# Pooled values in tiles of 112 and 32 partitions, a one-pass pooling of queries, and a new written order in an attention and mixture-of-experts kernel

## The chip, the cores and the metric

The kernel runs on one core of a Trainium2 chip. A core has five engines with instruction queues of their own: TensorE (PE in the profile, its weight loads PEld), VectorE (DVE), ScalarE (ACT), GpSimd (POOL) and SyncE (SP), which here issues all transfers. The metric is the device time of one execution in microseconds; less is better.

## The reference

Two batches of eight heads, 576 positions, head size 64, go through an attention with two branches, then through two feed-forward layers over 1152 tokens of width 512.

```python
q_d, k_d, v_d = (t.reshape(B, H, 144, 4, D).mean(axis=3) for t in (q, k, v))   # pooled by 4
out_d = softmax(q_d @ k_d.T / 8) @ v_d                                          # 144 x 144, no mask
out_up = np.repeat(out_d, 4, axis=2)
scores = np.where(abs(i - j) < 4, q @ k.T / 8, -1e9)                            # local window
x = (out_up + softmax(scores) @ v)            # -> tokens x 512
h = x @ w_in;  x = (h * sigmoid(h)) @ w_out   # 512 -> 2048 -> 512
p = domain_probs / domain_probs.sum(-1)
out = sum over e of p[:, e] * (relu(x @ w1[e]) @ w2[e])   # four experts, 512 -> 1024 -> 512
```

## The kernel before

The work is one long list of small steps, and TensorE does nearly all of the arithmetic in it. Attention comes as sixteen **jobs**, numbered 0 to 15 in the order batch, query half, pair of heads; jobs 0 to 3 and 8 to 11 have 256 queries per head in four blocks of 64, jobs 4 to 7 and 12 to 15 have 320 in five. Each step of a job has a letter, and a letter with a number is a step of one job: S local scores (fp32 matmuls of 64 rows by 64 columns and a mask added by an identity matmul), x maximum and subtraction, e exponential, k and q pooling of keys and queries, D pooled scores, n and d their maximum and exponential, u sums, r and g normalising, T transposes of the weights, a their copy out of PSUM, v pooling of the values on POOL, V the products with values, o the copy of the pooled part, f the sum of both branches, h and l the rounded high part and the low rest of the result (`xh`, `xl`), with which the products that follow work to nearly fp32 accuracy. The pooled queries past the last block are done per batch in one tail job (tp, tD, nt, dt, rt, gt, tT, ta).

In V the pooled keys are contracted, 144 of them. Before the change they lie as two halves of 72 partitions: `vg` is loaded as 72 rows of 4 KB, POOL adds four neighbours (two operations) into `vd`, and V contracts the halves kh = 0 and kh = 1 one after the other into the same PSUM columns, for each of two heads: four calls, each two fp32 passes (L483), before the calls of the local part (L487, 70 rows).

The weights of the first feed-forward layer come as 32 **pieces** of 512 KB (s0 to s31), of an encoding that three engines decode and split: A on ACT (two instructions, or one with the second, B, on DVE: `LOW_ON_DVE`), C on DVE, w the rounded copy (ACT, or DVE by `WHI_ON_DVE`), L the rest on POOL. Pieces 0 to 7 feed the first products (M and G, with th, gf, gh and gl after them), pieces 8 to 15 the second (H). The first token chunk (256 tokens) needs jobs 0 to 3, and its products H0 fill TensorE while jobs 4 to 7 are still on their way. `G1_0_0`, the first product of the second chunk, needs jobs 4 to 7. The experts' layer comes afterwards.

What sets the order: a scheduler by priorities, but over it the table `WRITTEN`, which gives for each engine a list of steps and adds an order between neighbours in it. An engine runs its instructions in that order and waits at the first that is not ready. Transfers are issued by SP in the order of the list as well, at most eight being under way, since they go round eight semaphores. Each step's PSUM tile is scarce: local scores have two, the transposes and V one each, products three.

Of the kernel before, what the change touches and what calls it, by code (L numbers as in the profile page):

```python
# [57 lines left out]
LOW_ON_DVE = (0, 3, 9, 13)  # L58
WHI_ON_DVE = (3, 4)
# [4 lines left out]
def attention_moe_kernel(ctx, tc, kqa, kqb, qtl, va, vb, w64, w1d, w2d, dpr, out):  # L64
# [350 lines left out]
    def down_scores(j):  # L415
        i = PE.matmul(out=j.ps[:, 352:352 + SD], lhsT=j.qd.rearrange("p a b -> p (a b)"), rhs=kd[j.b, j.hp],
                      start=True, stop=True)
        mark(f"D{j.i}", i)
        after(i, j.group)
# [27 lines left out]
    def trans(j):  # L447
        nb = j.nb
        if j.c == 1 and j.hp == 0:
            atd[j.b] = ac.tile([72, 2, NH, 80], F32, tag="atd1", name="atd1")  # L450
# [377 lines left out]
    def outputs(e, ci, ch, p):  # L828
# [36 lines left out]
        """S0 S1 D0 D1 S2 T0 S3 T1 V0 D2 D3 V1 M0 T2 V2 M1 T3 S4 V3 M2 D4 S5 M3 tD G0_3_0 G0_3_1 D5 G0_3_2 G0_3_3
        G0_4_0 G0_4_1 G0_4_2 T4 G0_4_3 G0_5_0 G0_5_1 G0_5_2 G0_5_3 G0_6_0 G0_6_1 G0_6_2 G0_6_3 S6 S7 tT G0_7_0
        G0_7_1 G0_7_2 G0_7_3 D6 V4 T5 H0_0_0 H0_1_0 D7 T6 V5 H0_2_0 H0_0_1 H0_1_1 H0_2_1 H0_0_2 H0_1_2 H0_2_2
        H0_0_3 V6 H0_1_3 H0_2_3 H0_0_4 H0_1_4 H0_2_4 H0_0_5 H0_1_5 T7 H0_2_5 H0_0_6 H0_1_6 H0_2_6 H0_0_7 H0_1_7
        H0_2_7 H0_3_0 H0_3_1 V7 H0_3_2 H0_3_3 H0_3_4 H0_3_5 H0_3_6 H0_3_7 G1_0_0 G1_0_1 G1_0_2 G1_0_3 G1_1_0
        G1_1_1 G1_1_2 G1_1_3 G1_2_0 G1_2_1 G1_2_2 G1_2_3 G1_3_0 G1_3_1 G1_3_2 G1_3_3 G1_4_0 G1_4_1 G1_4_2 G1_4_3  # L870
        G1_5_0 G1_5_1 G1_5_2 G1_5_3 G1_6_0 G1_6_1 G1_6_2 G1_6_3 G1_7_0 G1_7_1 G1_7_2 G1_7_3""",
# [226 lines left out]
```

## Time and profile before

| | |
|---|---|
| Runs of the kernel before, us | 675.71, 665.71, 662.03 (median 665.71) |
| Profiled execution | 659.74 us, of it span 657.7 us |
| Mean granted TensorE clock | 0.994 |
| Busy share: PE, PEld, DVE, ACT, POOL | 96%, 94%, 64%, 50%, 37% |

The span is what the profiler saw from the first to the last instruction; 2.04 us of the execution lie around it. All times of rows below count from the start of the span. Busy shares are means over stages with different limits, so the stages have to be looked at one by one.

### The profile page before, as it was taken

How to read it: one execution, taken by the hardware profiler on the slowest of the kernel's cores; microseconds unless marked ns; L12 is line 12 of the kernel's file. 1: busy time of each engine (PE TensorE's matmuls, PEld its weight loads, DVE VectorE, ACT ScalarE, POOL GpSimd, SP SyncE). 2: the span in 40 equal slices, each digit the busy share in tenths (PEclk: the TensorE clock that was granted, in tenths of full speed). 3: DMA queues.
4: the chain of work that ended last, by engine and by line, in shares of the span. 5: the costliest groups of instructions: out<-in, count | busy, mean ns of one | idle time of the engine just before them, and what ended most of it. 6: DMA issues, size and time to landing. Idle time of an engine off the chain costs nothing.

```text
span 657.7 us, 13693 instructions
## 1 busy us (share of the span) xinstructions
PE 630.2 (96%) x5484; PEld 616.3 (94%) x5484; DVE 418.8 (64%) x862; ACT 327.6 (50%) x744; POOL 245.3 (37%) x345
## 2 busy tenths in 40 slices
PE   4788999999999999999999999999999999999995
PEld 3677899999999999999999999999999999999995
DVE  6698465655545545766558956668954679755434
ACT  4789654568845434363345633346533356433321
POOL 5554651114510001653456322645522564333210
PEclk9899999999999999999999999999999999999998
DMA  9986512106612200240004310014300020000001
GB/s 260 328 283 181 170 54 73 26 5 196 191 59 65 65 1 1 65 161 1 1 1 129 97 33 2 1 34 129 97 1 1 1 65 1 1 33 33 1 33 50
DMA packets 16928, 48.17 MB, mean 73 GB/s; under 512 B 2976, under 2 KB 4256, under 8 KB 16864
## 3 DMA queue, kind: packets, MB, share of 16 engines
q1 hardware_dynamic: 16864, 47.29, 23.4%
q8 instruction: 43, 0.70, 0.5%
q14 instruction: 21, 0.17, 0.1%
HBM read 44.93 MB, written 2.36 MB: 72 GB/s over the span
## 4 chain that ended last, share of the span: by engine, by line
PE 79%; DMA 11%; DVE 3%; ACT 3%; POOL 2%; issue 1%; SPq 0%; ACTq 0%; POOLq 0%; DVEq 0%
PE mm L565 50%; PE p L794 26%; DMA stg<-in_w_dram 4%; DMA vg<-in_va_dram 2%; DMA acc<-in_kqa_dram 2%; DMA acc<-in_w_dram 2%; DMA qt<-in_qtl_dram 1%; DVE dec L230 1%; ACT stg L228 1%; PE t L455 1%; POOL vg L330 1%; ACT dec L222 1%; DMA kq<-in_kqa_dram 1%; PE o L487 1%; DVE acc L822 1%
## 5 line engine op out<-in xcount | busy, mean ns | idle before, releaser
L565 PE MATMUL mm<-xh,wbuf 128*128 128x256 f32 (+2 forms) x1280 | 263.8, 293 | 2.6 <-DVE gf L586 2.3
L565 PEld LDWEIGHTS mm<-xh,wbuf 128*128 128x128 f32 x1280 | 208.2, 188 | 4.1 <-DVE gf L586 3.3
L565 PE MATMUL mm<-xl,wbuf 128*128 128x256 f32 (+2 forms) x640 | 186.9, 292 | 0.0
L776 POOL TENSOR_TENSOR r<-r 128x128 f32<-128x128 f32 x160 | 95.3, 608 | 177.6 <-ACT r L770 136.2
L779 DVE TENSOR_TENSOR h<-r,h 128x384 fp32r<-128x384 f32 (+1 forms) x128 | 91.9, 719 | 64.5 <-ACT h L778 64.2
L778 ACT ACTIVATE h<-r 128x384 fp32r<-128x384 f32 (+1 forms) x128 | 73.7, 578 | 93.7 <-POOL r L776 54.2
L565 PEld LDWEIGHTS mm<-xl,wbuf 128*128 128x128 f32 x640 | 120.3, 188 | 0.0
L565 PE MATMUL mm<-gh,wbuf 128*128 128x256 f32 (+2 forms) x512 | 103.3, 295 | 0.3 <-DVE gf L586 0.2
L794 PE MATMUL p<-wext,h 128*128 128x256 f32 x672 | 89.4, 276 | 0.0
L565 PEld LDWEIGHTS mm<-gh,wbuf 128*128 128x128 f32 x512 | 82.2, 188 | 1.2 <-ACT acc L635 0.4
L794 PE MATMUL p<-wbuf,h 128*128 128x256 f32 x672 | 82.7, 276 | 0.0
L794 PEld LDWEIGHTS p<-wext,h 128*128 128x128 f32 x672 | 82.4, 188 | 0.0
L794 PEld LDWEIGHTS p<-wbuf,h 128*128 128x128 f32 x672 | 79.4, 188 | 0.0
L565 PE MATMUL mm<-gl,wbuf 128*128 128x256 f32 (+2 forms) x256 | 74.1, 292 | 0.0
L776 DVE TENSOR_TENSOR r<-r 128x128 f32<-128x128 f32 x96 | 39.3, 409 | 35.6 <-ACT r L770 31.2
L770 ACT ACTIVATE r<-mm 128x512 f32<-128x512 f32 x48 | 28.6, 597 | 65.3 <-PE mm L565 65.0
L565 PEld LDWEIGHTS mm<-gl,wbuf 128*128 128x128 f32 x256 | 48.1, 188 | 0.1
L592 DVE TENSOR_TENSOR gl<-gf,gh 128x256 fp32r<-128x256 f32 (+2 forms) x64 | 34.6, 543 | 17.9 <-ACT gh L591 17.5
L240 POOL TENSOR_TENSOR wbuf<-dec,wbuf 128x512 fp32r<-128x512 f32 x24 | 32.0, 1350 | 33.8 <-ACT wbuf L239 32.3
L591 ACT ACTIVATE gh<-gf 128x256 fp32r<-128x256 f32 (+2 forms) x64 | 28.1, 442 | 21.6 <-DVE gf L586 20.7
L822 DVE SCALAR_TENSOR_TENSOR acc<-p,pr,acc 128x256 f32<-128x256 f32 (+1 forms) x63 | 36.1, 604 | 3.5 <-PE p L794 3.0
L586 DVE SCALAR_TENSOR_TENSOR gf<-th,mm 128x256 f32<-128x256 f32 (+2 forms) x64 | 28.5, 451 | 14.9 <-ACT th L585 13.9
(138 smaller groups left out, 895.8 us busy)
## 6 DMA issues: line engine op xcount, KB each, us to landing
stg<-in_w_dram SPq DMA_DIRECT2D x25, 512.0 KB
kst<-in_w2d_dram SPq DMA_DIRECT2D x16, 512.0 KB
kst<-in_w1d_dram SPq DMA_DIRECT2D x12, 512.0 KB
acc<-in_w_dram SPq DMA_DIRECT2D x7, 512.0 KB
kq<-in_kqb_dram SPq DMA_DIRECT2D x8, 323.0 KB
kq<-in_kqa_dram SPq DMA_DIRECT2D x6, 419.0 KB
stg<-in_w1d_dram SPq DMA_DIRECT2D x4, 512.0 KB
vw<-in_vb_dram SPq DMA_DIRECT2D x8, 180.0 KB
```

The costliest lines, as they stand in the source:

```text
L222: first = ACT.activation(out=d, in_=v[:, :, 1].bitcast(F32), func=ACTF.Prelu, scale=2.0 ** -112, alpha=2.0 ** 32)
L240: mark(f"L{4 * u + j}", POOL.tensor_tensor(out=l[:, c], in0=d, in1=h[:, c].bitcast(F32), op=ALU.subtract))
L565: ins = [PE.matmul(out=ps, lhsT=l, rhs=r, start=(first and i == 0), stop=(last and i == n - 1)) for i, (l, r) in enumerate(pairs)]
L586: mark(f"gf{c}_{ft}", DVE.scalar_tensor_tensor(out=gf[:, 0:n], in0=th[:, 0:n], scalar=1.0, in1=ps[:, 0:n], op0=ALU.add, op1=ALU.mult))
L591: latest[ACT] = mark(f"gh{c}_{ft}", ACT.activation(out=gh[ft][:, 0:n], in_=gf[:, 0:n], func=ACTF.Copy))
L592: latest[DVE] = mark(f"gl{c}_{ft}", DVE.tensor_tensor(out=gl[ft][:, 0:n], in0=gf[:, 0:n], in1=gh[ft][:, 0:n].bitcast(F32), op=ALU.subtract))
L770: ACT.activation(out=r[:, 0:4].rearrange("p s t -> p (s t)"), in_=ps[:, 0:512], func=ACTF.Relu)
L776: latest[eng] = eng.tensor_tensor(out=r[:, o], in0=r[:, a], in1=r[:, b], op=op)
L778: ACT.activation(out=h, in_=r[:, part], func=ACTF.Copy)
L779: latest[DVE] = DVE.tensor_tensor(out=l, in0=r[:, part], in1=h.bitcast(F32), op=ALU.subtract)
L794: ins = [PE.matmul(out=ps, lhsT=x, rhs=y, start=(opens and k == 0 and i == 0), stop=(k == 3 and i == n - 1), skip_group_check=True) for i, ...
L822: DVE.scalar_tensor_tensor(out=o, in0=ps, scalar=p, in1=o, op0=ALU.mult, op1=ALU.add)
```

## The change

1. **Values.** `vg` and `vd` get 128 partitions. Of the first 72-row half of the load, the rows are cut in two halves of 2 KB that go to neighbouring partitions: rows 0 to 55 make partitions 0 to 111 (half 0), rows 56 to 71 make partitions 96 to 127 (half 1). That is two transfers for one, four POOL operations for two, and in V a call of 112 rows, then one of 32 rows, for each head. The exponential d writes its columns in the matching order, and the transposes of the pooled weights (L457, L470) become 128 columns wide.
2. **Queries of jobs 0 to 3.** One reduction over 128 partitions instead of two over 64; the pooled scores D of these jobs are two matmuls of 64 rows by 64 columns instead of one 128 by 128 with zeros in it.
3. **Who rounds what.** `LOW_ON_DVE` shrinks from pieces 0, 3, 9, 13 to piece 0; `WHI_ON_DVE` goes from 3, 4 to 2, 6, 9, 14, 15; a new table `WHI_ON_POOL` names 0, 3, 14.
4. **Order.** The load list and the four engine lists of `WRITTEN` are new.

```diff
-LOW_ON_DVE = (0, 3, 9, 13)
-WHI_ON_DVE = (3, 4)
+LOW_ON_DVE = (0,)
+WHI_ON_POOL = (0, 3, 14)
+WHI_ON_DVE = (2, 6, 9, 14, 15)
...
             if 4 * u + j in WHI_ON_DVE:
                 mark(f"w{4 * u + j}", DVE.tensor_copy(out=h[:, c], in_=d))
+            elif 4 * u + j in WHI_ON_POOL:
+                mark(f"w{4 * u + j}", POOL.tensor_copy(out=h[:, c], in_=d))
...
-            i = load(f"vg{j.i}", j.vg, va[j.b, j.hp, :, 0:1024])
+            for p, h, a in ((slice(0, 112), 0, slice(0, 56)), (slice(96, 128), 1, slice(56, 72))):
+                i = load(f"vg{j.i}", j.vg[p, 128 * h:128 * h + 128],
+                         va[j.b, j.hp, a, 0:1024].rearrange("p (k x) -> p k x", k=2))
...
-        for h in range(2):
-            p = slice(64 * h, 64 * h + 64)
-            mark(f"q{j.i}", DVE.tensor_reduce(out=j.qd[p, h], in_=q4[p], axis=AX.X, op=ALU.add))
+        mark(f"q{j.i}", DVE.tensor_reduce(out=j.qd, in_=q4, axis=AX.X, op=ALU.add))
...
-            mark(f"v{j.i}", fold(j.vg), padd(vf, j.vg[:, :, 0], j.vg[:, :, 1]))
+            for p, h in ((slice(0, 112), 0), (slice(96, 128), 1)):
+                g = j.vg[p, 128 * h:128 * h + 128]
+                mark(f"v{j.i}", fold(g), padd(v[p, h], g[:, :, 0], g[:, :, 1]))
...
+        if j.i < 4:
+            for h in range(2):
+                p = slice(64 * h, 64 * h + 64)
+                i = PE.matmul(out=j.ps[p, 352:352 + SD], lhsT=j.qd[p], rhs=kd[j.b, j.hp][p], start=True, stop=True)
...
-            mark(f"T{j.i}", PE.transpose(t2[0:72, 1 + kh], j.ed[:, 72 * kh:72 * kh + 72], ident))
+            mark(f"T{j.i}", PE.transpose(t2[:, 1 + kh], j.ed[:, 16 * kh:16 * kh + 128], ident))
...
-            for kh in range(2):
-                r = j.atd[:, kh, h, :] if j.c == 0 else atd[b][:, kh, 2 * hp + h, :]
-                mark(f"V{j.i}", PE.matmul(out=o[p, 320:320 + nd], lhsT=v[:, kh, p], rhs=r, start=(kh == 0), stop=(kh == 1)))
+            for kh, g in enumerate((slice(0, 112), slice(96, 128))):
+                r = j.atd[g, kh, h, :] if j.c == 0 else atd[b][g, kh, 2 * hp + h, :]
+                mark(f"V{j.i}", PE.matmul(out=o[p, 320:320 + nd], lhsT=v[g, kh, p], rhs=r, start=(kh == 0), stop=(kh == 1)))
...
-        """S0 S1 D0 D1 S2 T0 S3 T1 V0 D2 D3 V1 M0 T2 V2 M1 T3 S4 V3 M2 D4 S5 M3 tD G0_3_0 G0_3_1 D5 G0_3_2 G0_3_3
+        """S0 S1 D0 D1 T0 S2 V0 D2 S3 T1 M0 V1 T2 D3 S4 V2 M1 T3 S5 D4 V3 M2 T4 tD M3 D5 G0_3_0 G0_3_1 G0_3_2
...
-        """v0 v1 L0 L1 v2 v3 L2 L3 L4 p4 L5 L6 tp p5 L7 L8 L9 L10 p6 p7 L11 L12 L13 L14 L15""",
+        """v0 w0 L0 v1 v2 v3 L1 L2 w3 L3 p4 tp L4 L5 p5 L6 L7 L8 L9 p6 L10 L11 p7 L12 L13 w14 L14 L15""",
```

On TensorE the order of the first jobs before is this (L389 and L396 are S, L416 is D, L455 and L457 T, L483 and L487 V; tiles in these rows are named s scores, t transposed weights, o output):

```order
L416 MATMUL s<-kd,qbd_102 128x144
L416 MATMUL s<-kd,qbd_103 128x144
L389 MATMUL s<-kq_f 64x70 x8
L396 LDWEIGHTS ident_100
L396 MATMUL s<-mask,ident_100 128x280
L455 MATMUL t_233<-ident,sm 70x128 x4
L457 MATMUL t_234<-ident,ed 72x128 x2
L389 MATMUL s<-acc 64x70 x8
```

In the changed kernel the same place on TensorE reads so (L394 and L401 are S, L424 D, L467 and L469 T, L495 and L499 V):

```order
L424 MATMUL s<-kd,qs_102 64x144 x2
L424 MATMUL s<-kd,qs_103 64x144 x2
L467 MATMUL t_239<-ident,sm 70x128 x4
L469 MATMUL t_240<-ident,ed 128x128 x2
L394 MATMUL s<-kq_f 64x70 x8
L401 LDWEIGHTS ident_100
L401 MATMUL s<-mask,ident_100 128x280
L495 MATMUL o<-atd_249,vd 64x64 x4
L499 MATMUL o<-at,vw 64x64 x8
```

T0 has moved ahead of S2, and V0 ahead of S3, which is the first step to need the fourth load of keys and queries. A little later, likewise, S4 has come to stand ahead of V2, M1 and T3, behind which it stood.

On ScalarE before, this is the place at the end of the first batch: the two instructions of piece 14, then parts of pieces 16, 15 and 17, w14, o6, g7, w15, h6, a part of piece 18, and a7 (L458 to L465):

```order
L222 ACTIVATE dec<-stg_618 128x512
L228 ACTIVATE stg_618<-stg_618 128x512
L228 ACTIVATE stg_755<-stg_755 128x512
L222 ACTIVATE dec<-acc 128x512
L228 ACTIVATE acc<-acc 128x512
L228 ACTIVATE stg_823<-stg_823 128x512
L239 ACTIVATE wbuf<-dec 128x512
L490 ACTIVATE od<-o 128x80
L445 ACTIVATE ed<-ed,st 128x144
L239 ACTIVATE wbuf<-dec 128x512
L499 ACTIVATE xh<-o 128x320
L228 ACTIVATE stg_855<-stg_855 128x512
```

In the changed kernel the place on ScalarE between a6 and a7 holds gh0_6 and gh0_7 (L603), parts of pieces 16, 17 and 18 (L223, L229), g7 (L457) and o6 (L502):

```order
L603 ACTIVATE gh_648<-gf 128x256
L603 ACTIVATE gh_646<-gf 128x256
L229 ACTIVATE stg_769<-stg_769 128x512
L229 ACTIVATE stg_837<-stg_837 128x512
L457 ACTIVATE ed<-ed,st 128x144
L223 ACTIVATE dec<-stg_769 128x512
L229 ACTIVATE stg_869<-stg_869 128x512
L502 ACTIVATE od<-o 128x80
L470 ACTIVATE at<-t_1085 70x512
```

The copies w14 and w15 have left ScalarE, and piece 15 is done there well before; the parts of pieces 16 and 17 now come behind it.

On GpSimd the changed kernel has two of the rounding copies (CAST, L240), of pieces 0 and 3, among the values' pooling (L336) and the subtractions L (L243):

```order
L336 TENSOR_TENSOR vg_f_157<-vg_f_157 112x128x2
L336 TENSOR_TENSOR vd<-vg_f_157 112x128
L336 TENSOR_TENSOR vg_f_157<-vg_f_157 32x128x2
L336 TENSOR_TENSOR vd<-vg_f_157 32x128
L240 CAST wbuf<-dec 128x512
L243 TENSOR_TENSOR wbuf<-dec,wbuf 128x512
```

Before, the pooling was two rows of 72 partitions, and no CAST stood on GpSimd; no third one does now, for piece 14 stands in both tables and VectorE's is asked first.

## Rows read from the trace of the kernel before

**Rows 1.** The page, part 1: busy time of each engine.

```profile
PE 630.2 (96%) x5484; PEld 616.3 (94%) x5484; DVE 418.8 (64%) x862; ACT 327.6 (50%) x744; POOL 245.3 (37%) x345
```

**Rows 2.** Busy time by stage: stretch, its length, engines, then clock, DMA share, GB/s.

```profile
core 0: us, PE busy (x) PEld busy (x) DVE busy (x) ACT busy (x) POOL busy (x), PEclk, DMA share, GB/s
0.00:70.00 70.00, 51.05 (x588) 43.45 (x588) 53.06 (x134) 53.43 (x135) 38.49 (x57) 0.98 0.82 253
70.00:143.00 73.00, 72.75 (x809) 67.68 (x805) 42.04 (x120) 39.66 (x119) 20.71 (x43) 1.00 0.25 68
143.00:180.00 37.00, 35.92 (x257) 35.30 (x257) 21.91 (x35) 30.43 (x62) 18.43 (x14) 1.00 0.56 171
```

**Rows 3.** Waits of TensorE, 0 to 180 us: total, times, longest.

```profile
PE s L389 <- DMA kq<-in_kqa_dram: 4.2, 1, 4.2
PE s L389 <- DVE s L439: 3.6, 1, 3.6
PE mm L565 <- DVE gf L586: 2.5, 5, 1.0
```

**Rows 4.** TensorE in time: start, length, instruction, idle before it.

```profile
39.68 0.38 PE L565 MATMUL mm<-xh,wbuf 128*128 128x256 f32 x1 [0.43 <-DVE gf L586]
...
58.99 0.38 PE L565 MATMUL mm<-gh,wbuf 128*128 128x256 f32 x1 [0.17 <-DVE gf L586]
...
75.82 0.30 PE L565 MATMUL mm<-xh,wbuf 128*128 128x320 f32 x1
```

**Rows 5.** The chain that ended last, 105 to 123 us: start, length, what.

```profile
106.02 0.39 PE o L483 x8
106.41 0.47 PE o L487 x16
...
121.42 0.43 PE o L483 x8
121.85 0.58 PE o L487 x20
```

**Rows 6.** Stretches of 5 us while first loads run; columns as rows 2.

```profile
10.00:15.00 5.00, 1.36 (x18) 1.21 (x19) 4.65 (x15) 2.85 (x8) 2.20 (x3) 1.00 1.00 280
15.00:20.00 5.00, 4.54 (x54) 3.56 (x52) 3.77 (x8) 2.81 (x7) 2.89 (x3) 1.00 1.01 247
20.00:25.00 5.00, 3.15 (x46) 2.83 (x41) 4.23 (x15) 4.52 (x14) 2.46 (x4) 1.00 1.00 341
```

**Rows 7.** SyncE in time: the issue that had waited for job 4's load.

```profile
27.78 0.33 SPq L131 DMA_DIRECT2D vw<-in_vb_dram  x1
```

**Rows 8.** VectorE in time: pooling of queries, second decoding step, rounding copy.

```profile
4.21 0.84 DVE L359 TENSOR_REDUCE qbd<-kq 64x64 f32<-64x256 f32 x2 [3.35 <-POOL mask L267]
...
9.22 0.43 DVE L225 TENSOR_SCALAR stg<-stg 128x512 int32<-128x512 int32 x1 [0.19 <-DMA stg<-in_w_dram]
...
27.01 0.42 DVE L237 CAST wbuf<-dec 128x512 fp32r<-128x512 f32 x1
```

**Rows 9.** ScalarE in time.

```profile
15.07 0.66 ACT L228 ACTIVATE stg<-stg 128x512 int32<-128x512 uint16 x1
...
16.86 0.63 ACT L239 ACTIVATE wbuf<-dec 128x512 fp32r<-128x512 f32 x1
...
65.34 0.68 ACT L228 ACTIVATE stg<-stg 128x512 int32<-128x512 uint16 x1 [1.01 <-DMA stg<-in_w_dram]
```

**Rows 10.** From A5's start to a7's end on ScalarE; columns as rows 2.

```profile
28.81:69.31 40.50, 34.53 (x394) 30.30 (x392) 32.26 (x77) 36.34 (x94) 21.92 (x28) 0.96 0.75 234
```

**Rows 11.** GpSimd in time: pooling of values, a subtraction, pooling of queries.

```profile
7.46 1.04 POOL L330 TENSOR_TENSOR vg_f<-vg_f 72x512 f32<-72x512 f32 x1 [2.53 <-DMA vg_f<-in_va_dram]
8.58 0.64 POOL L330 TENSOR_TENSOR vd<-vg_f 72x256 f32<-72x256 f32 x1
...
14.44 1.29 POOL L240 TENSOR_TENSOR wbuf<-dec,wbuf 128x512 fp32r<-128x512 f32 x1
...
32.21 0.42 POOL L330 TENSOR_TENSOR kq<-kq 128x128 f32<-128x128 f32 x1 [1.07 <-PE s L389]
```

More of the change, by code (lines that the diff above doesn't have):

```diff
@@ L257, in attention_moe_kernel @@
     mask = ac.tile([128, 6, WIN], BF16, name="mask")
+    qs = [ac.tile([128, BQ], F32, name=f"qs{i}") for i in range(2)]
     qbd = [ac.tile([128, 2, BQ], F32, name=f"qbd{i}") for i in range(2)]
@@ L415, in down_scores @@
     def down_scores(j):
[L416 to L419, printed above, removed]
+        if j.i < 4:
+            for h in range(2):
+                p = slice(64 * h, 64 * h + 64)
+                i = PE.matmul(out=j.ps[p, 352:352 + SD], lhsT=j.qd[p], rhs=kd[j.b, j.hp][p], start=True, stop=True)
+                mark(f"D{j.i}", i)
+                after(i, j.group)
+        else:
+            i = PE.matmul(out=j.ps[:, 352:352 + SD], lhsT=j.qd.rearrange("p a b -> p (a b)"), rhs=kd[j.b, j.hp],
+                          start=True, stop=True)
+            mark(f"D{j.i}", i)
+            after(i, j.group)
     def tail_scores(l):
@@ L449, in trans @@
         if j.c == 1 and j.hp == 0:
-            atd[j.b] = ac.tile([72, 2, NH, 80], F32, tag="atd1", name="atd1")
+            atd[j.b] = ac.tile([128, 2, NH, 80], F32, tag="atd1", name="atd1")
         t1 = t_p.tile([128, 4, 128], F32, tag="t1", name="t1")
@@ L462, in trans @@
         else:
-            j.atd = ac.tile([72, 2, 2, 64], F32, tag="atd0", name="atd0")
+            j.atd = ac.tile([128, 2, 2, 64], F32, tag="atd0", name="atd0")
             dst = j.atd
-        mark(f"a{j.i}", ACT.activation(out=dst, in_=t2[0:72, 1:3].rearrange("p a (h q) -> p a h q", h=2), func=ACTF.Copy))
+        mark(f"a{j.i}", ACT.activation(out=dst, in_=t2[:, 1:3].rearrange("p a (h q) -> p a h q", h=2), func=ACTF.Copy))
     def tail_trans(l):
@@ L867, in attention_moe_kernel @@
[L867 to L871, printed above, removed]
@@ L872, in attention_moe_kernel @@
-        """tab e0 e1 A0 d0 d1 w0 g0 g1 A1 a0 w1 e2 e3 o0 a1 d2 h0 d3 A2 g2 o1 A3 h1 w2 a2 g3 A4 o2 A5 a3 h2 A6 e4
-        o3 w5 w6 h3 d4 A7 A8 th0_0 th0_1 g4 e5 th0_2 gh0_0 gh0_1 w7 th0_3 w8 gh0_2 dt0 d5 A9 gt0 th0_4 A10 w9 g5
-        gh0_3 a4 w10 gh0_4 A11 A12 e6 ta e7 th0_5 th0_6 w11 o4 d6 a5 h4 g6 A13 th0_7 gh0_5 d7 w12 o5 gh0_6 gh0_7
-        w13 h5 a6 A14 A15 w14 o6 g7 w15 h6 a7 ya0_0 ya0_1 ya0_2 o7 h7 ya0_3 th1_0 gh1_0 th1_1 gh1_1 th1_2 gh1_2
-        th1_3 gh1_3 th1_4 gh1_4 th1_5 gh1_5 th1_6 gh1_6 th1_7 gh1_7""",
@@ new lines, in attention_moe_kernel @@
+        H0_0_3 H0_1_3 V5 H0_2_3 T6 H0_0_4 H0_1_4 H0_2_4 H0_0_5 H0_1_5 H0_2_5 V6 T7 H0_0_6 H0_1_6 H0_2_6 H0_0_7
+        H0_1_7 H0_2_7 H0_3_0 H0_3_1 H0_3_2 H0_3_3 V7 H0_3_4 H0_3_5 H0_3_6 H0_3_7 G1_0_0 G1_0_1 G1_0_2 G1_0_3
+        G1_1_0 G1_1_1 G1_1_2 G1_1_3 G1_2_0 G1_2_1 G1_2_2 G1_2_3 G1_3_0 G1_3_1 G1_3_2 G1_3_3 G1_4_0 G1_4_1 G1_4_2
+        G1_4_3 G1_5_0 G1_5_1 G1_5_2 G1_5_3 G1_6_0 G1_6_1 G1_6_2 G1_6_3 G1_7_0 G1_7_1 G1_7_2 G1_7_3""",
+        """tab e0 A0 e1 d0 g0 d1 A1 a0 e2 g1 o0 h0 d2 a1 A2 w1 g2 o1 e3 A3 a2 A4 h1 d3 g3 o2 A5 e4 h2 a3 w4 w5 d4
```

42 lines of the change are left out of this document (23 added, 19 removed).

## The prediction

> **What bounds the kernel now.** I read the page's busy times first: TensorE is busy for 630.2 of 657.7 us [rows 1], so 27.5 us of idle time is all that any reordering can win. The table by stage says where it lies [rows 2]: 70.00 − 51.05 = 18.95 us in the first 70 us, 0.25 us in the next 73, 1.08 us up to 180. From 70 us on TensorE is the bound, and what is added to it there is added to the end. Before that it waits. The waits name causes of several kinds [rows 3]: 4.2 us for the very first load, which no order shortens, 3.6 us for VectorE's normalising of job 0, 2.5 us in five pieces for VectorE's first gate step. So the most that this change can win is 18.95 − 4.2 = 14.8 us, 2.2% of the profiled execution's 659.74 us, and only with a TensorE that never waits after its first load.
>
> The feeder that is nearest to full is ScalarE. Between the start of A5 (28.81) and the end of a7 (69.31), the last copy that TensorE needs of the first batch, it is busy 36.34 of 40.50 us [rows 10]: 4.16 us idle, 1.01 us of it in one wait for a load that stands ahead of w14, g7 and w15 [rows 9]. Gains on VectorE and GpSimd count only where they let ScalarE start earlier or wait less. After a7, TensorE has 6.5 us to `G1_0_0` at 75.82 [rows 4], and from there on runs without a gap worth counting.
>
> **The change part by part.**
>
> *Loads of values.* From 10 to 20 us, where three of the four vg loads and most of the 72-row vw loads run, 280 and 247 GB/s arrive; from 20 to 25 us, with loads of 128 rows, 341 [rows 6], at a DMA share of 1.0 in both. At 341 the 2.64 MB of those 10 us would take 7.7, so the narrow loads cost at most 2.3 us; vg carries two thirds of the narrow bytes (288 KB against 144 each), which leaves 1.5 us to this edit. The lower end is below nothing: vg now takes two of the eight places under way and four more issues at about 0.33 us [rows 7], in a row where SP is not the bound; I put it at −0.5. I take 1.0 us earlier for the loads behind the fourth vg, nearer to the upper end because the engines' share was full. The Trainium skill (DMA: Bandwidth & Descriptors, why a DMA increments its semaphore by 16) says that a transfer uses the largest number of engines up to 16 that divides both row counts: 12 for 72 rows, 14 for 56 pairs of rows, 16 for 32. By it the busiest engine's share of a vg falls from 24 to 20 KB, an estimate of a sixth less; by that share the loads would come 0.5 us earlier instead of 1.0, and the sum would be 660.6. No row here separates engines.
>
> *VectorE.* A pair of query reductions takes 0.84 us for 64 partitions each [rows 8]; one over 128 partitions has as many elements in a lane as one of them, so 0.42: −1.7 us for four jobs. Second decoding steps of pieces 3, 9, 13 leave (−3 × 0.42), five rounding copies stand for two (+3 × 0.42): nothing.
>
> *ScalarE.* It takes three decoding steps (+3 × 0.66) and hands over five copies (−5 × 0.63) [rows 9]: −1.2 us in all, but all of that before A5. Inside the stretch from A5 to a7, w4 comes in and four copies go (6, 9, 14, 15), two decoding steps come in, and a first step of piece 16 has moved ahead of a7: −3 × 0.63 + 3 × 0.66 = +0.1, nothing. So the stretch is 36.3 us of work again.
>
> *GpSimd.* A pooling of values was 1.04 + 0.64 us; in two parts it is twice the price of 256 and of 128 elements, 2 × (0.64 + 0.42) = 2.1 [rows 11]: +0.4 us for each of eight, hidden while GpSimd is idle for 31.5 of the first 70 us [rows 2]. No row shows its copy of 512 elements. Above, it can't reasonably exceed the two-input subtraction of that size, 1.29; below, VectorE's 0.42. I take 1.0, and it stands where w on ScalarE took 0.63: w0 then reaches M0 well before h0 and l0 do, and w3 is needed only by M3. The third copy doesn't happen on GpSimd: piece 14 is in both tables, and VectorE's is asked first. That costs VectorE 0.42, counted above. Without this cover (L0 late for M0) the price would be some 0.6 us once.
>
> *The order, walked.* I went through both lists with durations of like rows. Job 0 is normalised before the second exponential maximum and the third query, so T0 comes some 3 us earlier; V0 no longer stands behind S3 and its load, and M0 starts near 19.5. Next S4 now stands ahead of V2, M1 and T3. It needs job 4's load, which by SP's next issue had landed at 27.78 [rows 7]; with the loads 1.0 us earlier it lands near 26.7, about when V2 could start anyway, for V has one PSUM tile and waits for l1. A5 then starts near 28.1, 0.7 us earlier. From there ScalarE finds its inputs ready in nearly all places: pieces 12 to 15 land long before their turn, and the parts of pieces 16 and 17 come after piece 15 and at a time when their loads are in. With no idle time a7 would end at 28.1 + 36.3 = 64.4, 4.9 us earlier; with all of the old 4.16 us, 0.7 us earlier. My walk leaves out the hand-overs between engines, so I take half of the idle time as won: 0.7 + 2.1 = 2.8, rounded to 3.0 us, which TensorE passes on to `G1_0_0` since its own part after a7 is as long as before. On the way it finds `G0_3_0` about 2 and the third product of H0 several us earlier than 39.68 and 58.99 [rows 4], so TensorE isn't the late one in this stage.
>
> *The two calls in V.* This is added on TensorE. A V block of 8 passes with 64 columns took 0.39 us, the block behind it, of the same 128-row by 64-column shape, 0.47 for 16 [rows 5]: 0.029 a pass, so 8 cost 0.235 and entering the shape 0.155. With 80 columns, 0.43 − 8 × 0.036 = 0.14. So a change of tile shape costs about 0.14 to 0.155 us. Calls of 112 rows and of 32 now alternate, which is four changes in each V that weren't there. At 0.155 that is 0.6 us a job; at the low end some of it is the late second weight load, which a call of two passes doesn't suffer, and 0.1 remains: 0.4 us. Below that, nothing, if a 32-row call counts as no change of shape. I take 0.42. V4 to V7 lie where TensorE has slack while ScalarE is late; V8 to V15 lie after 70 us, on the bound: +8 × 0.42 = 3.4 us. The Trainium skill (TensorEngine Tiling (Array Packing), Tiling Modes, key properties) says that a change of tiling mode drains TensorE, and lists 32 rows as a mode apart from 128; no row here shows these two in turn, and by that rule the price isn't zero. The sum doesn't rest on it.
>
> *The rest.* D of jobs 0 to 3 is two small matmuls in quarters that don't overlap, in a time when TensorE waits; at worst it enters a shape once more, 4 × 0.15 us in slack. Wider transposes stream the same 128 columns of the identity. The changed column order of the exponential writes as many elements. For these I count nothing; if strided writes cost ScalarE a tenth of a microsecond each, eight of them lie in the stretch and take 0.8 from the gain.
>
> *Sum.* 659.74 − 3.0 + 3.4 = 660.1 us for a profiled execution. The runs shown lie higher: 662.03 and 665.71 and one far off; their median is 6.0 above the profile, the mean of the lower two 4.1. I take 4, nearer to the two runs that agree: **664 us**.
>
> **The rivals.**
>
> *V costs nothing more.* If a 32-row call behind one of 112 costs no change, 3.4 us come off, and with all idle time of ScalarE won another 1.9: 660.1 − 5.3 = 654.8, 659 as a median. For it: the call needs only the last quarter of the rows. Against it: each entry into another shape in the rows had a price. Chance 0.20.
>
> *V at its full price: slower.* The place is V8 to V15, the price 0.6 us each, 4.8 together, and V4 to V7 add 2.4 as soon as TensorE and not ScalarE is the late one. With the 3.0 won before, it decides from 3.0 / 8 = 0.38 us a job; with 0.7 won it ends at 659.74 − 0.7 + 7.2 = 666.2, 670 as a median. Chance 0.22.
>
> *S4 waits instead of V2.* If the loads aren't earlier, S4 stands until 27.8 with V2, M1 and T3 behind it, V2 begins 1.8 us later than in my walk, and o2, A5 and all of ScalarE's stretch follow: the 3.0 shrinks to 1.2, 661.9 and a median of 666. The doubled places under way speak for it, the bandwidth of rows 6 against it. Chance 0.18.
>
> *The order does what it looks like.* Nearly all waits vanish as well as V being cheap: up to 8 us, 652 profiled, 656. Chance 0.05; the forecast keeps 0.35.
>
> **How the numbers follow.** The likeliest case gives 664. The cases run from 656 to 670, and runs of one kernel spread by 662 to 676, so the range is 656 to 673. About 2% is what a measurement of this kernel can tell from no change: 13 us. To be faster by that, TensorE would have to lose nearly all of its 14.8 us, 0.04; to be slower by that needs V at more than its full price and nothing won, 0.05; within it 0.91.
>
> **What would show it.** In the profile after, V blocks of 8 passes should take 0.75 to 1.0 us instead of 0.39 to 0.43, and TensorE's busy time between 70 and 143 us should grow by about 3. The CAST on GpSimd should show its price, twice. ScalarE from A5 to a7 should have 2 us of idle time left, no wait for a load ahead of w14, and `G1_0_0` should start near 72.8. I'm wrong if V blocks stay at 0.4, if S4 has a wait over 2 us for its load, or if `G1_0_0` comes before 69 or after 75.

## The result, and the profile after

The changed kernel takes 671.26 us (median of 9 runs, 668.47 to 683.04), the kernel before beside it 662.03 (9 runs, 658.42 to 675.71). The ratio is 1.0135, 95% interval 1.0099 to 1.0171: about 9 us slower, beyond what the runs scatter. Forecast was 664, no change. In some executions a whole run goes some per cent slower, whatever the kernel; the ratios leave those out and the medians don't, so trust the ratio where the two disagree.

The profiled execution took 669.33 us, its span is 667.5, against 659.74 and 657.7. The page's busy times come first, then the table by stage (length, engines, clock, DMA share, GB/s):

```profile
PE 645.1 (97%) x5492; PEld 626.3 (94%) x5492; DVE 419.4 (63%) x858; ACT 326.0 (49%) x742; POOL 248.7 (37%) x363
```

```profile
0.00:70.00 70.00, 56.28 (x563) 46.39 (x564) 50.95 (x127) 49.43 (x127) 39.97 (x66) 0.95 0.80 251
70.00:143.00 73.00, 73.00 (x731) 66.18 (x729) 41.52 (x115) 38.19 (x112) 22.88 (x52) 1.00 0.24 69
143.00:180.00 37.00, 35.90 (x300) 34.70 (x300) 20.45 (x38) 26.45 (x59) 13.09 (x10) 1.00 0.38 118
```

TensorE is busy for 14.9 us more than in [rows 1], while the span grew by 9.8. In the first 70 us its idle time fell from 18.95 [rows 2] to 13.72, and yet it came out of them later, as will be seen. From 70 to 143 us it has no idle time at all. So look for what TensorE does longer. The chain that ended last, at the places of [rows 5] (start, length, what; L495 is V, L499 the products of vw):

```profile
110.81 1.02 PE o L495 x8
111.84 0.61 PE o L499 x16
...
127.82 1.12 PE o L495 x8
128.94 0.73 PE o L499 x20
```

V and the products of vw behind it took 0.39 + 0.47 = 0.86 us and 0.43 + 0.58 = 1.01. Now it is 1.63 and 1.85: 0.77 and 0.84 more for each job. Eight jobs lie behind 70 us: 4 × 0.77 + 4 × 0.84 = 6.4 us, two thirds of the loss.

The rest is in front of `G1_0_0`. TensorE in time, 16 to 80 us (start, length, instruction, idle before it):

```profile
16.38 1.66 PE L495 MATMUL o<-atd,vd 112*64 112x64 f32 x8 [1.10 <-ACT atd L477]
...
27.82 0.83 PE L394 MATMUL s<-kq 64*64 64x70 f32 x20 [0.70 <-DMA kq<-in_kqb_dram]
...
29.83 1.65 PE L495 MATMUL o<-atd,vd 112*64 112x64 f32 x8 [0.92 <-DVE xl L512]
31.41 1.12 PE L499 MATMUL o<-at,vw_f 70*64 70x64 f32 x16
32.46 0.58 PE L577 MATMUL mm<-xh,wbuf 128*128 128x256 f32 x1
...
44.43 0.39 PE L577 MATMUL mm<-xh,wbuf 128*128 128x256 f32 x1 [0.60 <-DVE gf L598]
...
79.34 0.31 PE L577 MATMUL mm<-xh,wbuf 128*128 128x320 f32 x1
```

`G1_0_0` is the last row: 79.34, against 75.82 [rows 4]. It is 3.5 us late, and 3.5 + 6.4 = 9.9 is the 9.8 of the span but for a tenth. Ahead of it, V0 to V7 and the products of vw behind them take TensorE 15.9 us, read job by job from start to start; in before they took 7.6. All its other work up to there takes 49.7 us (49.3 before), and its idle time is 5.2 us less. So the longer V's 8.4 us and 0.4 of other work, less 5.2 of idle time, are the 3.5. That is the account of one profile, and single profiles differ at this place by as much (e11 below, as fast as before, has `G1_0_0` at 79.66); the cause has to come from the experiments.

V2 (29.83) is a row to look at: it waits 0.92 us for l1, and it and the products of vw last until 32.46, where M1 starts: 2.63 us, where before they took 0.86. ScalarE stands behind it:

```profile
32.58 0.22 ACT L502 ACTIVATE od<-o 128x64 f32<-128x64 f32 x1 [1.59 <-PE o L499]
32.70 0.66 ACT L223 ACTIVATE dec<-acc 128x512 f32<-128x512 f32 x1
```

```profile
32.70:71.57 38.87, 36.64 (x373) 32.02 (x374) 32.37 (x76) 35.48 (x94) 20.58 (x23) 0.96 0.66 215
```

A5 begins at 32.70 and a7 ends at 71.57; in [rows 10] it was 28.81 and 69.31. The stretch itself became shorter, 38.87 us instead of 40.50.

What answers to the other rows: five-microsecond stretches as in [rows 6], GpSimd's groups as in [rows 11] (busy, mean ns | idle), a query reduction as in [rows 8], the waits as in [rows 3].

```profile
10.00:15.00 5.00, 3.43 (x27) 2.39 (x27) 3.84 (x12) 2.46 (x9) 1.88 (x2) 1.00 0.97 239
15.00:20.00 5.00, 3.90 (x37) 3.06 (x38) 2.98 (x8) 2.31 (x7) 4.29 (x9) 1.00 1.02 276
20.00:25.00 5.00, 5.00 (x54) 4.25 (x53) 3.63 (x10) 3.52 (x10) 2.63 (x5) 1.00 1.03 316
```

```profile
L336 POOL TENSOR_TENSOR vg_f<-vg_f 112x256 f32<-112x256 f32 x4 | 2.4, 612 | 4.0 <-DMA vg_f<-in_va_dram 3.8
...
L336 POOL TENSOR_TENSOR vg_f<-vg_f 32x256 f32<-32x256 f32 x4 | 2.4, 612 | 0.3
...
L336 POOL TENSOR_TENSOR vd<-vg_f 32x128 f32<-32x128 f32 x4 | 2.0, 492 | 0.3
...
L336 POOL TENSOR_TENSOR vd<-vg_f 112x128 f32<-112x128 f32 x4 | 1.6, 411 | 0.3
L240 POOL CAST wbuf<-dec 128x512 fp32r<-128x512 f32 x2 | 1.2, 610 | 2.7 <-DVE dec L231 2.7
```

```profile
4.31 0.42 DVE L363 TENSOR_REDUCE qs<-kq 128x64 f32<-128x256 f32 x1 [3.44 <-DMA kq<-in_kqa_dram]
```

```profile
PE s L394 <- DMA kq<-in_kqa_dram: 4.3, 1, 4.3
PE mm L577 <- DVE gf L598: 2.4, 3, 1.1
...
PE t L467 <- DVE sm L455: 1.3, 2, 1.1
```

### The profile page after: what moved, and what is told of

It reads as the page before. It is cut to its first block, busy times and chain, and to the rows that moved or that the text cites. A ratio compares the mean times of both kernels' runs of the same rounds, so it can differ in the third digit from the quotient of the medians.

```text
span 667.5 us, 13745 instructions
## 1 busy us (share of the span) xinstructions
PE 645.1 (97%) x5492; PEld 626.3 (94%) x5492; DVE 419.4 (63%) x858; ACT 326.0 (49%) x742; POOL 248.7 (37%) x363
## 4 chain that ended last, share of the span: by engine, by line
PE 88%; ACT 4%; DMA 4%; DVE 2%; issue 1%; SPq 1%; POOL 0%; ACTq 0%; POOLq 0%; DVEq 0%
PE mm L577 54%; PE p L806 26%; DMA stg<-in_w_dram 4%; PE o L495 2%; PE o L499 2%; PE s L394 1%; PE t L467 1%; ACT dec L223 1%; ACT stg L229 1%; SPq L132 1%; DVE acc L834 1%; PE s L428 1%; DVE dec L231 0%; PE s L401 0%; POOL wbuf L243 0%
## 5 line engine op out<-in xcount | busy, mean ns | idle before, releaser
L243 POOL TENSOR_TENSOR wbuf<-dec,wbuf 128x512 fp32r<-128x512 f32 x24 | 31.3, 1317 | 33.1 <-ACT wbuf L242 25.4
L603 ACT ACTIVATE gh<-gf 128x256 fp32r<-128x256 f32 (+2 forms) x64 | 28.0, 441 | 19.4 <-DVE gf L598 18.7
```

The source lines that it names most:

```text
L243: mark(f"L{4 * u + j}", POOL.tensor_tensor(out=l[:, c], in0=d, in1=h[:, c].bitcast(F32), op=ALU.subtract))
L603: latest[ACT] = mark(f"gh{c}_{ft}", ACT.activation(out=gh[ft][:, 0:n], in_=gf[:, 0:n], func=ACTF.Copy))
```

## Where V's time goes

The 80-column V of before, and then the products behind it, in time:

```profile
121.35 0.51 PE L483 MATMUL o<-atd,vd 72*64 72x80 f32 x8
121.68 0.76 PE L487 MATMUL o<-at,vw 70*64 70x64 f32 x20
```

From start to start that is 0.33 us; after, the same two rows stand at 127.75 and 128.87, 1.12 us apart. A V is four calls (two heads, two halves) of two passes each. The starts of its single matmuls, as ns from one to the next (the last number leads to vw), in before, in after and in two of the experiments below:

```
before                        13 107  13  56  13  56  13  56   =  327
after                        120 163 120 157 120 163 120 157   = 1120
calls by half (e4)             6 114   6 163   6 114   6 158   =  573
all calls of 32 rows (e11)    13 107  13  56  13  56  13 158   =  429
```

In before the passes start in pairs 13 ns apart: the two heads have different 64-column tiles, and they run side by side. After the first pair (120 ns to the next), a pair follows every 69 ns. That the two passes of a pair run at once, and not one behind the other, can be worked out from the rows of after: there a pass of 80 columns takes 120 ns to the second of its call and one of 64 columns 107 (V8 to V11), 13 ns for 16 columns. By that, 80 columns take some 65 ns (an estimate), so two passes in 69 ns can't stand in line. The gap inside a pair fits as well: 13 ns where two calls of one head are written ahead of the other head's first, 6 ns in e4, where it is one.

In after no pair is left. Each call stands alone between two changes of tile height: 120 ns from its first pass to its second, 160 to the next call. Four times 280 is the 1120. Two theories were to be told apart from this. A: the two tile heights in V cost 0.8 us a job, and that is nearly the whole loss. B: the new order, its loads and the copies on GpSimd cost the time.

## The experiments

Each ran in 5 rounds beside the kernel before. "V" is the 80-column V, start to start.

| run | time us | before us | ratio, 95% interval | span | V | `G1_0_0` |
|---|---|---|---|---|---|---|
| after | 671.26 | 662.03 | 1.0135 (1.0099–1.0171) | 667.5 | 1.12 | 79.34 |
| e1 72-row values, new order | 660.36 | 661.46 | 0.9982 (0.9952–1.0012) | 656.3 | 0.33 | 74.41 |
| e2 values part alone | 674.06 | 661.46 | 1.0173 (1.0135–1.0211) | 668.3 | 1.12 | 79.84 |
| e3 second call over 128 rows | 661.45 | 661.46 | 0.9995 (0.9972–1.0017) | 659.4 | 0.33 | 75.84 |
| e4 calls by half | 664.05 | 661.46 | 1.0037 (1.0014–1.0059) | 661.8 | 0.57 | 76.11 |
| e5 V2 ahead of S4 | 660.85 | 661.88 | 0.9980 (0.9953–1.0007) | 659.3 | 0.33 | 78.57 |
| e6 w14 on GpSimd | 663.66 | 661.88 | 1.0022 (0.9994–1.0049) | 659.8 | 0.33 | 76.66 |
| e7 queries alone | 662.26 | 661.88 | 0.9997 (0.9969–1.0024) | 660.9 | 0.33 | 77.12 |
| e8 two loads of 72-row values | 661.33 | 661.88 | 0.9992 (0.9967–1.0017) | 659.7 | 0.33 | 76.69 |
| e9 shape of 32 rows alone | 671.87 | 662.31 | 1.0161 (1.0130–1.0192) | 668.9 | 1.12 | 81.10 |
| e10 shape of 64 rows alone | 672.05 | 662.31 | 1.0160 (1.0133–1.0187) | 672.5 | 1.12 | 83.90 |
| e11 all calls of 32 rows | 662.23 | 662.31 | 1.0008 (0.9985–1.0032) | 662.8 | 0.43 | 79.66 |
| e12 e1 with TensorE's waits filled | 665.57 | 662.89 | 0.9957 (0.9927–0.9987) | 655.2 | 0.33 | 73.51 |

**e1.** All lines of the values part go back to one load, one pooling and calls of 72 rows; the rest of the change stays.

```diff
-            for kh, g in enumerate((slice(0, 112), slice(96, 128))):
-                r = j.atd[g, kh, h, :] if j.c == 0 else atd[b][g, kh, 2 * hp + h, :]
+            for kh in range(2):
+                r = j.atd[:, kh, h, :] if j.c == 0 else atd[b][:, kh, 2 * hp + h, :]
```

> The kernel after with the values part as before: one load and one pooling of 72 rows, two calls of 72 rows for each head in V; query reductions, rounding copies and written order stay as after. Theory A (the two tile shapes in V cost about 0.8 us a job and that is nearly the whole loss): V falls from 1.02 to 1.12 us back to 0.25 to 0.33 (start of V to start of the products of vw), and the time falls by 9 to 11 us below the kernel after, to within 2 us of the kernel before. Theory B (the new order, its loads and the copies on GpSimd cost the time): V falls all the same, but the time stays 6 us or more above the kernel before.

The 1.35% are gone. V in its profile:

```profile
120.03 0.51 PE L492 MATMUL o<-atd,vd 72*64 72x80 f32 x8
120.35 0.76 PE L496 MATMUL o<-at,vw 70*64 70x64 f32 x20
```

B falls: order, queries and copies are all still in this kernel. (The loads and the pooling of the values went back with the calls; e3 keeps them.)

**e2.** The opposite: the values part, as in the diff of the change, in the kernel before.

> The kernel before with the values part alone: two loads, poolings and calls of 112 and 32 rows, the old order, query reductions and copies. Theory A: V takes 1.0 to 1.1 us instead of 0.25 to 0.33; V8 to V15 add 6.3 us at the end, the earlier eight up to as much again, less what lies in TensorE's slack: 7 to 11 us slower than the kernel before. Theory B: at most 3 us slower.

The whole loss is there without the new order; at 1.7% it is slightly above what was expected.

**e3.** The values part stays with all its loads, poolings and wide transposes. Only the tile height of the second call changes:

```diff
-            v = vd[j.b, j.hp] = a4.tile([128, 2, 128], F32, tag="vd", name="vd")
+            v = vd[j.b, j.hp] = vds[j.hp]
...
+        for t in vds:
+            DVE.memset(t[0:96, 1], 0.0)
...
-            for kh, g in enumerate((slice(0, 112), slice(96, 128))):
+            for kh, g in enumerate((slice(0, 112), slice(0, 128))):
```

> The kernel after, but the second call of each head runs over all 128 rows, with zeros in the 96 rows of the pooled values that it doesn't use (fixed tiles, set to zero once), so that all calls of V have one tile shape. Theory A: V takes 0.25 to 0.35 us, and the time falls by 9 to 11 us below the kernel after, the same as with 72 rows within 2 us. Theory B: V is as short, the time falls by 3 us at most.

```profile
123.13 0.51 PE L498 MATMUL o<-atd,vds 112*64 112x80 f32 x8
123.46 0.76 PE L502 MATMUL o<-at,vw 70*64 70x64 f32 x20
```

Four times as many rows in the second call, 96 of them zeros, and V falls from 1.12 to 0.33 us and the time to that of before: by the two ratios the turn between heights costs about 9 us (1.0135 against 0.9995). The loads and poolings of 112 and 32 rows cost nothing that shows at the end.

**e4.** The same four calls as in after, in another sequence:

```diff
-        for h in range(2):
-            p = slice(64 * h, 64 * h + 64)
-            for kh, g in enumerate((slice(0, 112), slice(96, 128))):
+        for kh, g in enumerate((slice(0, 112), slice(96, 128))):
+            for h in range(2):
+                p = slice(64 * h, 64 * h + 64)
```

> The kernel after, with the four calls of V in another sequence: 112 rows for both heads, then 32 rows for both heads; two changes of shape in place of four, and calls of one shape stand next to each other for two column tiles. Theory A1 (the loss is that two heads no longer run side by side, and the changes): V takes 0.51 to 0.56 us, half of now, and the time falls by 4 to 6 us below the kernel after. Theory A2 (only the changes cost, heads never ran side by side): V takes 0.8 us or more, the time falls by 2 us or less. Theory B: no change of the time.

```profile
123.57 0.64 PE L495 MATMUL o<-atd,vd 112*64 112x80 f32 x8
124.14 0.80 PE L499 MATMUL o<-at,vw 70*64 70x64 f32 x20
```

A1 holds, a little outside its numbers: V takes 0.57 us (0.56 at most was expected), and by the ratios the time falls by about 6.5 us below after (4 to 6 expected). The pairs are back (6 ns in the table of starts), and half of the changes are gone. This splits the price. With pairs kept, two changes cost 573 − 327 = 246 ns, 0.12 us each. The way from there to after, 1120 − 573 = 547 ns, is two more changes, and with them the heads one after the other instead of side by side. If those two changes cost 0.12 us each as well, 0.3 us is left for the lost pairing; that is an estimate, for no run has four changes with its pairs kept.

**e9, e10, e11.** The kernel before, with nothing but the rows of the calls changed (e9 below; e10 has `slice(0, 64)` for the second call, e11 `slice(32, 64)` for both). They leave rows out of the sums, so only their times are of use.

```diff
-                r = j.atd[:, kh, h, :] if j.c == 0 else atd[b][:, kh, 2 * hp + h, :]
+                g = slice(0, 72) if kh == 0 else slice(32, 64)
+                r = j.atd[g, kh, h, :] if j.c == 0 else atd[b][g, kh, 2 * hp + h, :]
```

> The kernel before, with one thing changed: the second call of each head in V runs over 32 of the 72 rows (the other 40 rows of that half are left out of the sum). Loads, poolings, transposes and order are those of before. Theory A: V takes 1.02 us (64 columns) and 1.12 us (80 columns) instead of 0.28 and 0.33; V8 to V15 alone add 6.3 us, the other eight part of as much: 7 to 11 us slower, the same as the whole values part. The rival: part of the 12 us that the values part cost comes from its two loads, its poolings and wide transposes; then this is 5 us slower at most.

> As the run with 32 rows, but the second call of each head runs over 64 of the 72 rows (8 are left out). If any two heights of tile in turn cost this (64 rows are a shape apart from 72), V takes 1.0 to 1.1 us and the time is within 2 us of the run with 32 rows. If it is calls of 32 rows that cost, V stays at 0.28 to 0.33 us and the time within 2 us of before.

> As the run with 32 rows, but both calls of each head run over the same 32 rows (the other 40 are left out of both sums), so that the shape changes only on the way into V and out of it. Theory A (the turn between shapes costs, not the small shape): V takes 0.28 to 0.5 us, and the time is within 3 us of before. The rival (a call of 32 rows is slow in itself): V takes 0.9 us or more, 7 us or more slower.

TensorE in e9, e10 and e11:

```profile
129.20 1.19 PE L484 MATMUL o<-atd,vd 72*64 72x80 f32 x8
130.32 0.80 PE L488 MATMUL o<-at,vw 70*64 70x64 f32 x20
```

```profile
138.50 1.20 PE L484 MATMUL o<-atd,vd 72*64 72x80 f32 x8
139.62 0.80 PE L488 MATMUL o<-at,vw 70*64 70x64 f32 x20
```

```profile
125.52 0.50 PE L484 MATMUL o<-atd,vd 32*64 32x80 f32 x8
125.95 0.80 PE L488 MATMUL o<-at,vw 70*64 70x64 f32 x20
```

Less work, and 1.6% more time: e9 leaves rows out and is as slow as the whole values part. It isn't the 32 rows, since 64 in turn with 72 cost the same, and 32 rows in all calls cost 0.10 us for V's one change on the way out and nothing that shows in the time. What costs is the turn between two heights. Not every other number of rows is another height: 112 and 128 rows in turn (e3), and 72 rows with 70 behind them (before), keep the pairs and V's 0.33 us.

**e7, e6, e8: the other parts.** e7 puts the query part alone into the kernel before; e6 takes piece 14 out of VectorE's table in e1, so that its copy does run on GpSimd (348 instructions there instead of 347); e8 splits each vg of e1 into two loads.

```diff
-WHI_ON_DVE = (2, 6, 9, 14, 15)
+WHI_ON_DVE = (2, 6, 9, 15)
```

```diff
-            i = load(f"vg{j.i}", j.vg, va[j.b, j.hp, :, 0:1024])
+            for a in (slice(0, 56), slice(56, 72)):
+                i = load(f"vg{j.i}", j.vg[a], va[j.b, j.hp, a, 0:1024])
```

> The kernel before with the query part alone: one reduction of 128 partitions in place of two of 64 for jobs 0 to 3, and their D as two matmuls in quarters. VectorE is spared 4 times 0.42 us. If VectorE's chain is what TensorE waits for in the first 20 us (3.6 us in the wait for job 0's normalising), the end comes 0.8 to 1.7 us earlier than before; if that time is lost again in ScalarE's stretch behind 28.8 us, within 0.4 us of before.

> The kernel of the first experiment, with piece 14 taken out of VectorE's table, so that its rounding copy does run on GpSimd. As the forecast has it the place of this copy decides nothing: within 0.5 us of the first experiment, GpSimd's busy time 0.6 us longer and VectorE's 0.4 shorter. The rival: the copy holds up L14 and L15 on GpSimd and with them the products of their pieces, 0.6 us or more slower.

> The kernel of the first experiment, but each load of pooled values goes as two DMAs, of 56 and of 16 rows into the same tile; all else stays. In the profiles kq4 came at 26.4 us with one load of 72 rows and at 27.8 with loads of 112 and 32 rows, in the same order of loads. If the number of loads under way does that (two of eight places for each vg), kq4 comes 1.0 to 1.5 us later than in the first experiment, S4 with it, and the end 1 to 3 us later. If it is the shape of the loads (112 and 32 partitions), kq4 stays at 26.4 and the time within 0.5 us.

None differs from before beyond its interval. For e7 that interval reaches from 2.1 us faster to 1.6 us slower, so the 0.8 to 1.7 us of its first case aren't seen, but not excluded either. e6 was expected within 0.5 us of e1; its ratio is 0.4% above e1's, some 2.6 us, with intervals that overlap, so what this copy costs stays open. e8's question got no answer: its S4 began at 26.73, about as early as in e1 (26.46), so two loads for one didn't delay it there. But e6, which differs from e1 in w14 alone, began S4 at 28.35, and e3 at 28.81. The landing of this load differs by 2 us between executions, more than the loads' shape or number could be shown to do.

**e5.** V2 stood behind S4 and its load, so it was put ahead in e1's lists ("T2 D3 V2 S4 M1" on TensorE, f2 ahead of x4, h2 ahead of e4).

> The kernel of the first experiment (72-row values, new order), with V2 written ahead of S4 instead of behind it, and what hangs on V2 brought forward on the other engines (f2 ahead of x4, h2 ahead of e4). There TensorE waited 2.21 us for S4's load with V2 ready behind it, and ScalarE then 1.53 us for V2. Theory C (this wait holds back ScalarE, and through it TensorE, until 70 us): V2 starts near 26.9 instead of 28.0 us, A5 1.0 us earlier, a7 and the end 0.8 to 1.2 us earlier than in the first experiment. Theory D (the wait is made up for by other idle time before 70 us): within 0.4 us of the first experiment.

```profile
28.19 0.66 PE L492 MATMUL o<-atd,vd 72*64 72x64 f32 x8 [2.69 <-DVE xl L509]
```

Inconclusive: in this execution V2 had to wait for l1 and came no earlier than e1's (28.02), so C's case didn't arise. The time is e1's.

**e12.** The table by stage of e1 shows the other thing that stretched V2: TensorE's granted clock. 25 to 30 and 30 to 35 us, in before, after and e1 (columns as in the first table by stage):

```profile
25.00:30.00 5.00, 3.28 (x41) 2.90 (x40) 3.73 (x10) 4.36 (x10) 2.68 (x3) 0.89 1.03 342
30.00:35.00 5.00, 4.95 (x61) 3.93 (x59) 2.88 (x7) 3.50 (x10) 2.16 (x4) 0.77 0.93 320
```

```profile
25.00:30.00 5.00, 2.40 (x33) 1.65 (x31) 3.49 (x10) 4.17 (x11) 3.87 (x4) 0.88 1.04 380
30.00:35.00 5.00, 5.00 (x36) 4.33 (x36) 3.42 (x9) 2.42 (x6) 2.06 (x7) 0.50 0.90 243
```

```profile
25.00:30.00 5.00, 3.54 (x47) 2.99 (x48) 3.37 (x11) 2.45 (x8) 3.89 (x8) 0.67 0.99 339
30.00:35.00 5.00, 5.00 (x54) 4.26 (x55) 2.28 (x6) 3.52 (x8) 0.79 (x1) 0.64 0.91 293
```

In after the whole stretch from 30 to 35 us is granted half (1.2 GHz, the lower of the two levels), following one in which TensorE was idle for 2.6 of 5 us. So products that nobody needs were put into e1's waits for D3 and S4:

```diff
+        if j.i == 4:
+            for k in range(18):
+                mark("F0" if k < 6 else "F1", PE.matmul(out=j.ps[:, 0:280], lhsT=ident16, rhs=mask[:, 0:4].rearrange("p m c -> p (m c)"),
+                                                        start=True, stop=True))
...
-        T2 D3 S4 V2
+        T2 F0 D3 F1 S4 V2
```

> The kernel of the first experiment, with 18 mask products of 280 columns (about 0.12 us each, 2.1 together) added on TensorE where it waits for inputs: 6 ahead of D3, 12 ahead of S4, into the PSUM tile that S4 then begins anew, so the result is the same. In the profile of the first experiment TensorE waited there 1.4 and 2.2 us, and its granted clock was 0.67 and 0.64 in the stretches of 25 to 30 and 30 to 35 us, some 3 us of work done at half speed. Theory E (idle time there brings the lower clock, and the lower clock holds back V2 and with it ScalarE): the granted clock is 0.85 or more in both stretches, V2 and M1 take their full-speed times, and the end comes 1 to 2 us earlier than in the first experiment. Theory F (the time there is set by loads and ScalarE, whatever TensorE's clock): the clock rises or not, and the time stays within 0.7 us. If the added products delay D3 or S4 instead, it is up to 1 us slower.

```profile
25.00:30.00 5.00, 4.91 (x69) 3.86 (x70) 3.54 (x10) 3.97 (x12) 4.09 (x7) 1.00 1.01 365
30.00:35.00 5.00, 4.44 (x66) 3.72 (x64) 4.76 (x13) 4.42 (x12) 3.01 (x5) 1.00 0.92 281
```

```profile
25.40 1.60 PE L389 MATMUL s<-mask,ident 128*128 128x280 bf16 x12
27.02 0.83 PE L395 MATMUL s<-kq 64*64 64x70 f32 x20
...
28.18 0.46 PE L496 MATMUL o<-atd,vd 72*64 72x64 f32 x8
28.43 0.67 PE L500 MATMUL o<-at,vw_f 70*64 70x64 f32 x16
29.03 0.39 PE L578 MATMUL mm<-xh,wbuf 128*128 128x256 f32 x1
```

The clock stays at full, V2 and its products take 0.85 us, and `G1_0_0` comes at 73.51, the earliest of all. The ratio to before is 0.9957, and of all these kernels it is the only one whose interval lies wholly below 1, by 0.1 to 0.7%. Against e1 the gain is 0.9 us in the profiles' `G1_0_0` and about 1.7 us by the ratios (1 to 2 expected), but the two intervals overlap. So E is shown in its clock, and its price is likely but not shown.

## Why the prediction was wrong, point by point

**The step that failed is the price of the two calls in V, and with it the slack in which V4 to V7 were to lie.** The prediction found the right place and a right cause (a change of tile height for each call), and took 0.42 us a job, with 0.6 as the upper end. Measured were 0.77 to 0.84. Four changes alone, at the 0.12 that e4 shows, would have been 0.49, inside its bounds. What was left out is that before, the two heads ran side by side. [Rows 5] held one half of the sign: 0.029 us a pass of 64 columns, where one that is alone takes 0.107 to the next of its call in after (0.120 with 80 columns). By taking the mean of a group as the price of one pass, the working took for a cheap pass what was two at a time. Its reason for the low price, that a call of two passes doesn't suffer from a late second weight load, isn't borne out: in after, at the full clock, a call takes those 107 or 120 ns from its first pass to its second. The Trainium skill (TensorEngine Tiling (Array Packing), Tiling Modes, key properties) states both halves: that different tiles can load weights and multiply in parallel, and that a change of mode drains TensorE. The starts above agree with both; the prediction weighed the second alone. Behind 70 us this term gave 6.4 us instead of 3.4.

V4 to V7 were put at nothing, as slack. In after TensorE's last idle time ahead of `G1_0_0` worth counting ends at 60.8 us (67.0 before), so V5 to V7 (62.76, 67.96 and 75.97) lay on the bound as well: 3 × 0.84 = 2.5 of the 3.5 us. The part after a7, which was to be as long as before, is 7.77 us instead of 6.51, with no idle time in it and V7 at its new length. So V costs at the end ahead of 70 us too, which the likeliest case left out; the rival of the full price had these jobs in it.

**The 3.0 us of the order didn't come.** The stretch on ScalarE came near to what was worked out: 1.6 us shorter than before where 2.1 were taken (35.48 us busy against 36.3, 3.4 idle against 2). But A5 began at 32.70, not 28.1. At first the walk held: V0 starts 2.8 us earlier than in before (16.38 against 19.21). But it and the products of vw take 2.64 us instead of 0.86, and M0 starts at 21.97, not near 19.5 (23.53 before). Of A5's 4.6 us, 1.1 are S4, which had its load at 27.82 and not at 26.7. 1.8 are V2 and its products, 2.63 us instead of 0.86: the changes (0.77) and the clock at its lower level (the rest). In the last 1.7 lies V2's wait of 0.92 us for l1, which the walk didn't have; what the others are isn't traced. So V0 to V3 were not free either.

With the changes gone and all else as in after (e3), `G1_0_0` stands at 75.84, before's 75.82; with 72-row values and the new order it came between 74.41 and 78.57 (e1, e5, e6, e8). The order wins nothing that these runs could tell from zero; the ratios of those four lie between 0.998 and 1.002. The profile of e1 hints at where its gain goes. Ahead of `G1_0_0` TensorE is idle for 14.7 us there instead of 18.95, but busy for 59.7 instead of 56.9. Its granted clock is at the lower level for six whole microseconds (27 to 33), in before for three (29 to 32). In e12, where it stays at the full level, TensorE is busy for 59.7 us with 2.1 us of useless products in it, so about 57.6 without them. So in these profiles most of the idle time that the order removes comes back as slower work; single profiles don't prove it.

**The loads** were to be 1.0 us earlier. 239 and 276 GB/s arrive from 10 to 20 us, 280 and 247 before, and job 4's load isn't earlier. What e8 and e6 show is only that this term, at either sign, is lost in the 2 us by which executions differ.

**VectorE and GpSimd** went as worked out. A query reduction takes 0.41 to 0.42 us for 128 partitions; in e7 no gain from the 1.7 us saved could be seen at the end. Pooling a vg of jobs 0 to 3 takes 0.61 + 0.41 us for its 112 rows and 0.61 + 0.49 for its 32, together 2.13, forecast 2.1. The copy on GpSimd takes 0.61 us, not 1.0, inside its bounds. Two copies and not three run there, and no wait for a load stands in ScalarE's stretch any more.

**What it said would show it.** V was to be 0.75 to 1.0 us and is 1.02 to 1.12; TensorE's busy time from 70 to 143 us couldn't grow by 3, since only 0.25 was idle: what is added there moves the end instead. `G1_0_0` after 75 was named as a sign of being wrong, and it came at 79.34; S4's wait, another sign if over 2 us, was 0.70. `G0_3_0` was to come about 2 us ahead of 39.68 and came at 44.43.

**The rivals.** The one that came true is V at its full price, 0.22, with 670 us; it had the place right and 0.6 for 0.8. The S4 rival was right that the load doesn't come earlier. The range, 656 to 673, holds the measured time; the likeliest case didn't. That 664 lies no farther than 7.3 us off is partly luck: the 4 us put between profile and median are 1.9 in after (671.26 − 669.33) and 2.3 in before, and the profile's own forecast, 660.1, was 9.2 us short. Nor is 2% what it takes to tell two kernels apart here: the interval is 0.4% to either side.

The sum, made with the measured terms: 659.74 + 3.5 (`G1_0_0`) + 6.4 (V8 to V15) = 669.6, profiled 669.33. Both terms are read from the profile after, so this shows that nothing is left over; that V is the cause is shown by e1 to e4 and e9 to e11.

## What to carry to other kernels

Before a small matmul is cut into calls of different heights, look at the starts of single matmuls in the trace: where they come in pairs, two column tiles run at once, and calls that change height within each of them, one tile behind the other, run singly (V 1.12 us for 0.33 here). If the rows must be cut, keep one height by padding with zeros (here 96 of 128 rows were zeros, and free), or write all calls of one height next to each other. A gain in a start-up phase whose milestones differ by 2 us from execution to execution needs many runs to be shown, and one profile can't carry a walk of 3 us.

## What was not expected of the hardware

- A turn between 72 and 64 rows costs the same as one between 72 and 32 (V 1.12 us in both), though the first two differ by 8 rows only.
- V0 in after took 1.59 us from its start to that of the products behind it (16.38, the row above, to 17.96), V2's slow duration, in a stretch whose granted clock is shown as 1.00; it followed TensorE's idle time. So here a row's own duration told more than the clock column of its stretch.
- 18 useless products, 2.1 us of work, in waits of TensorE didn't delay S4: it began at 27.02, when its load was in (SyncE's next issue, which waits for the same load, came at 27.04). With them the granted clock was 1.00 from 25 to 35 us.
